# Longformer attention and a snake MLP on one core: the third block of w_in issued behind the casts, and batch 1's global rows turned a group sooner and placed ahead of w_out

## The chip, the cores and the metric

The kernel runs on one core of a Trainium2 chip. The metric is device microseconds of one execution. Before the change three runs gave 374.94 us as the median (374.66 to 376.61).

## The reference

For 8 batches of 8 heads, 576 positions and head dimension 64, attention is computed with a mask that keeps a band of 32 positions to either side, and all rows and columns of 8 global positions. Its output, turned to 4608 tokens of 512, goes through a two-layer network with a snake-like activation.

```python
scores = scale * np.matmul(q, k.transpose(0, 1, 3, 2))
mask = np.abs(pos[:, None] - pos[None, :]) <= window
mask = mask | is_global[:, None] | is_global[None, :]
attn = softmax(np.where(mask, scores, -1e9))     # in the reference written out
x = np.matmul(attn, v)                           # then (4608, 512)
h = x @ w_in                                     # (512, 2048)
g = h + np.sin(alpha * h) ** 2 / (alpha + 1e-9)
out = g @ w_out                                  # (2048, 512)
```

## The kernel before

**Stages.** The program is unrolled by hand, in an order written out in Python; each engine executes its instructions in that order. Attention of batch 0 comes first (`phase_a(0, None)`). Then for each batch b comes `gemm1(b)`, the first matrix product with its activation, and beside the attention of batch b+1 the second product of batch b, `gemm2(b)`, of which single matmuls are dealt out by `fill(n)`.

**Attention.** Keys lie in `KX[b % 2]` and queries in `QX[b % 2]`, both in a layout of 12 blocks of 48 positions, where each block also holds the 8 global keys, or 4 global queries to either side. For each of 4 pairs of heads (hp), three score groups of 4 blocks are computed (L741) into two PSUM buffers in turn (`ring`), exponentiated by ACT (L749) and masked by DVE (L752). Then follow the products with V (L783, key 0, into zn) and with ones (key 1, into zd), the inverse of the sums on ACT as a logarithm and an exponential (L809, L812), and DVE's normalisation (L815), which frees zn for the next pair. In batches 0 and 1 spare matmuls (`warm`, L545) are put between the scores. In batch 1 no matmul of `gemm2(0)` comes before the third pair (`LATE`).

**The first product.** `gemm1(b)` goes through 16 groups (nt) of 128 columns of `w_in`. A group is 8 matmuls (L990) into one of four PSUM places; for batch 0 the places are, in order, `nrdonrdonrdnrdon`, where n, r, d and o are zn, zr, zd and the two halves of zo. Then follow a sine on ACT (L1020), a square on ACT or DVE (L1024, L1026), and the sum on DVE into H (L1028), which frees the place. For batch 0 the squares of groups 1, 3, 5, 7 and 9 to 14 are on ACT. In groups 10 to 13 of batch 0, DVE also places keys and queries of batch 1's first two pairs of heads (`place`, L356 and L349); the other pairs' are placed by `place_rest` after the first pair of batch 1's attention.

**Global rows.** SP gathers the global rows of k, q and v for all batches (`gather`, L488), in float32 into parts of H. `turn_kq` (L697) transposes those of k and q on PE into `zo[1]`, and DVE copies them to `kTg` and `qTg` (L707). `cast_globals_v` (L695) casts those of v on POOL. `place_globals(b)` (L366) copies the global keys of batch b into KX, in 8 copies of 64x96, one for each pair and half, and the global queries into QX in 2 copies of 128x112; all these run on POOL. The attention of batch 1 reads both.

**POOL's queue.** POOL issues all transfers that cast to bfloat16: V (`load_v`, L393, four for each pair of heads), k and q to DRAM (`cast_qk`, L330; SP then transposes them back by DMA, L339, into `kt` and `qt`), `w_in` in four blocks of 512 columns (L410, block g serves groups 4g to 4g+3), and `w_out` in four quarters (L416, in the order in which `gemm2` uses them). Before the change its order after the start is: blocks 0 and 1 of `w_in` between the V loads of batch 0; `cast_qk(1)`; three memsets of batch 1's buffers; a 1x1 copy into `seen` which reads `kt` and so holds POOL until that transpose has landed (L1118); blocks 2 and 3 of `w_in` (L1119); half of batch 1's V; then, emitted at group 11 of `gemm1(0)`, `w_out`, the cast of V's global rows, `place_globals(1)`, the other half of batch 1's V, and after that `cast_qk(2)` and batch 2's V.

**SP's queue** has, in the same stretch: the gather of q, the two transposes of batch 1, the gather of v, and `load_vg`, which spreads the global rows of V (L402).

Of the kernel before, what the change touches and what calls it, by code (L numbers as in the profile page):

```python
# [18 lines left out]
NG = 8  # L19
KT = 48  # L20
# [227 lines left out]
def kernel(  # L248
# [12 lines left out]
    B, H, S, D = q.shape  # L261
# [3 lines left out]
    NT12 = S // KT  # L265
    NHP = H // 2
# [26 lines left out]
    KX = [main.tile([P, NHP, NT12, P], DT.bfloat16, name=f"KX{i}") for i in range(2)]  # L293
# [9 lines left out]
    kTg = main.tile([P, NHP, NG, B], DT.bfloat16, name="kTg")  # L303
# [21 lines left out]
    def cast_qk(b):  # L325

        cast[b] = []
        for src, name in ((k, "kd"), (q, "qd")):
            t = dramp.tile([P, H * S * D // P], DT.bfloat16, name=name)
            nc.gpsimd.dma_start(  # L330
                out=t[:], in_=src[b].rearrange("h s d -> (h s d)").rearrange("(p f) -> p f", p=P)
            )
            cast[b].insert(0, t)
# [31 lines left out]

    def place_globals(b):  # L366

        for hp in range(NHP):
            for t in range(2):
                rows = slice(t * D, (t + 1) * D)  # L370
                nc.gpsimd.tensor_copy(
                    out=KX[b % 2][rows, hp, :, t * D + KT : t * D + KT + NG],
                    in_=kTg[rows, hp, None, :, b].to_broadcast([D, NT12, NG]),
                )
        for y in range(2):
            nc.gpsimd.tensor_copy(
                out=globals_of(b, slice(0, P), y),
                in_=qTg[:, :, None, y::2, b].to_broadcast([P, NHP, 7, 4]),
            )
# [8 lines left out]
    def load_v(b, hps=range(NHP)):  # L388
        for hp in hps:
            for t in range(2):  # L390
                for y in range(2):
                    r = t * D + y * 24
                    nc.gpsimd.dma_start(  # L393
                        out=VX[b % 2][r : r + 24, hp, :, t * D : t * D + D],
                        in_=v[b, 2 * hp + t].rearrange("(i a y) d -> y a i d", a=24, y=2)[y],
                    )

    def load_vg(b):
        for h in range(H):
            t = h % 2  # L400
            src = VGb[b::B, h * D : (h + 1) * D] if b else VG0[h::H]
            nc.sync.dma_start(  # L402
                out=VX[b % 2][t * D + KT : t * D + KT + NG, h // 2, :, t * D : t * D + D],
                in_=src[:, None, :].to_broadcast([NG, NT12, D]),
            )

    def load_w_in(gs):
        for g in gs:
            cols = slice(g * DFF // 4, (g + 1) * DFF // 4)
            nc.gpsimd.dma_start(  # L410
                out=w_in[:, :, cols], in_=moe_w_in[:, cols].rearrange("(c p) n -> p c n", p=P)
            )

    def load_w_out():
        for g in range(4):
            nc.gpsimd.dma_start(  # L416
                out=w_out[:, 4 * g : 4 * g + 4, :],
                in_=moe_w_out[4 * g * P : (4 * g + 4) * P, :].rearrange("(t p) n -> p t n", p=P),
            )
# [21 lines left out]
    for half in range(2):  # L441
        for w, src in ((1, k), (0, q)):
            nc.gpsimd.dma_start(
                out=nat[w][D * half : D * half + HK],
# [23 lines left out]
    for t in (gidx8, gp64):  # L468
        nc.vector.memset(t[:].bitcast(DT.int32), 0)
    nc.sync.dma_start(  # L470
        out=g64[:],
# [4 lines left out]
    for t in (0, D):  # L476
        nc.sync.dma_start(out=gp64[t + KT : t + KT + NG], in_=global_idx[:, None])
        nc.sync.dma_start(
            out=gidx8[t + KT : t + KT + NG],
# [82 lines left out]
    load_w_in((1,))  # L562
    load_v(0, (3,))
    cast_qk(1)
    load_vg(0)
    gather(q, gq)

# [399 lines left out]
    def gemm1(b):  # L967


        xT = xTs[b]  # L970
        r0 = (b % 2) * S
        more = b == B - 1
        W = HALF + (NE if more else 0)
        hr = tc.alloc_tile_pool(name="hr", bufs=1, space=PSUM)
        hs = {}

        order = "nrdonrdonrdnrdon" if b == 0 else "nrd" * 5 + "n"

        def chunks(nt, cs):
            if nt not in hs:  # L980
                if order[nt] == "o":
                    hs[nt] = [(slice(e, e + 1), zo[e][:, None, :]) for e in range(2)]
                else:
                    h = {"n": zn, "d": zd}.get(order[nt]) or hr.tile([P, 2, 512], DT.float32, name="zr")
                    hs[nt] = [(slice(0, 2), h[:])]
            h = [ap[:, i] for es, ap in hs[nt] for i in range(es.stop - es.start)]
            for c in cs:
                for e in range(2):
                    lhsT = w_in[:, c, nt * P : (nt + 1) * P]
                    nc.tensor.matmul(  # L990
                        out=h[e][:, 0:W], lhsT=lhsT, rhs=xT[:, c, e, 0:W],
                        start=(c == 0), stop=(c == CT - 1), skip_group_check=True,
                    )

        on_act = (ON_ACT_FIRST, ON_ACT_SECOND, ON_ACT)[min(b, 2)]
        for nt in range(NT):
            if b < 2 and 10 <= nt < 14:
                for which, t, y in PLACES[2 * (nt - 10) : 2 * (nt - 9)]:
                    place(b + 1, which, t, y, nc.vector.tensor_copy, slice(0, NHP if b else 2))
            if b == 1 and nt in (3, 4):  # L1000
                square_x(0, nt - 3)
            if b == 0 and nt == 11:
                turn_kq()
            if b == 0 and nt == 11:

                load_w_out()
                cast_globals_v()
                place_globals(1)
                load_v(1, (2, 3))
                load_vg(1)  # L1010
            if nt == 0:

                for n in range(2):
                    chunks(n, range(CT - 1))
            chunks(nt, range(CT - 1, CT) if nt < 2 else range(CT))
            fill((GROUP_LATE if b == 1 else PER_GROUP)[nt])
            sb = spool.tile([P, 2, HALF + NE], DT.bfloat16, name="sb")
            s2 = spool.tile([P, 2, HALF + NE], DT.bfloat16, name="s2")
            for es, h in hs[nt]:
                nc.scalar.activation(  # L1020
                    out=sb[:, es, 0:W], in_=h[:, :, 0:W], func=AF.Sin, scale=alphaT[:, nt : nt + 1]
                )
            if nt in on_act:
                nc.scalar.activation(out=s2[:, :, 0:W], in_=sb[:, :, 0:W], func=AF.Square)  # L1024
            else:
                nc.vector.tensor_tensor(out=s2[:, :, 0:W], in0=sb[:, :, 0:W], in1=sb[:, :, 0:W], op=ALU.mult)  # L1026
            for es, h in hs[nt]:
                nc.vector.scalar_tensor_tensor(  # L1028
                    out=H2[:, nt, r0 : r0 + S].rearrange("p (e c) -> p e c", e=2)[:, es],
                    in0=s2[:, es, 0:HALF], scalar=recipT[:, nt : nt + 1], in1=h[:, :, 0:HALF],  # L1030
                    op0=ALU.mult, op1=ALU.add,
                )
            if more:
                nc.vector.scalar_tensor_tensor(
                    out=HG[:, nt, :].rearrange("p (x n) -> p x n", x=2),
                    in0=s2[:, :, HALF:W], scalar=recipT[:, nt : nt + 1], in1=hs[nt][0][1][:, :, HALF:W],
                    op0=ALU.mult, op1=ALU.add,
                )
        hr.release()
# [65 lines left out]
    def phase_a(b_att, b_moe):  # L1105
        def beside(at):

            if b_moe is None:
                if at == -1:
                    nc.vector.tensor_scalar(out=recipT[:], in0=alphaT[:], scalar1=1e-9, scalar2=None, op0=ALU.add)  # L1110
                    nc.vector.reciprocal(out=recipT[:], in_=recipT[:])
                if at == 0:
                    second_half()
                    nc.gpsimd.memset(VX[1][:].bitcast(DT.int32), 0)
                    nc.gpsimd.memset(QX[1][:].bitcast(DT.int32), 0)
                    nc.gpsimd.memset(KX[1][:].bitcast(DT.int32), 0)
                    turn_qk(1)
                    nc.gpsimd.tensor_copy(out=seen[:], in_=turned[1][1][0:1, 0:1])  # L1118
                    load_w_in((2, 3))  # L1119
                    load_v(1, (0, 1))  # L1120
                    gather(v, gv)
                return
            if 0 <= at < 2 and b_moe:
                square_x(b_moe, at)
            if b_att == 1 and at == 0:
                place_rest(1)
                place_rest(0)
            for which, t, y in places_at(b_att, at):
                place(b_att + 1, which, t, y, nc.vector.tensor_copy)
            if b_moe == 0 and at == 2:  # L1130
                turn_qk(2)

        if b_moe is not None:
            waiting.append(gemm2(b_moe))
        attention(b_att, beside)
# [77 lines left out]
```

## Time and profile before

| | |
|---|---|
| median of three runs | 374.94 us |
| profiled execution | 374.3 us |
| its span, first to last instruction | 372.6 us |
| mean granted PE clock | 0.986 |
| PE busy | 338.7 us (91%) |
| ACT busy | 293.9 us (79%) |
| DVE busy | 282.8 us (76%) |
| POOL busy | 138.3 us (37%) |
| `gemm1(0)`: first and last L990 matmuls start | 31.97 and 50.95 us |
| attention of batch 1: first scores | 54.05 us |
| `gemm1(1)`: first L990 matmuls | 71.67 us |

The span begins with the first instruction and ends with the last; the profiled execution's time is 1.7 us above it. Busy shares are taken over the whole span, though the stretch that the change touches lies between 23 and 75 us, and is read from the timelines, which merge neighbouring instructions of one kind: start, duration, engine, line, what is written and read, their number, and in brackets the idle time ahead of them and what ended it. A transfer's row on POOL is its issue; the time to its landing is counted from the issue's start: 6.1 and 8.6 us for blocks 2 and 3 of `w_in`, 5.9, 8.0, 9.7 and 12.0 us for the quarters of `w_out`, 7.2 and 9.1 us for the casts of k and q of batch 1.

### The profile page before, as it was taken

How to read it: one execution, taken by the hardware profiler on the slowest of the kernel's cores; microseconds unless marked ns; L12 is line 12 of the kernel's file. 1: busy time of each engine (PE TensorE's matmuls, PEld its weight loads, DVE VectorE, ACT ScalarE, POOL GpSimd, SP SyncE). 2: the span in 40 equal slices, each digit the busy share in tenths (PEclk: the TensorE clock that was granted, in tenths of full speed). 3: DMA queues.
4: the chain of work that ended last, by engine and by line, in shares of the span. 5: the costliest groups of instructions: out<-in, count | busy, mean ns of one | idle time of the engine just before them, and what ended most of it. 6: DMA issues, size and time to landing. Idle time of an engine off the chain costs nothing. (4 is left out here: it accounts for less than half of the span.)

```text
span 372.6 us, 8428 instructions
## 1 busy us (share of the span) xinstructions
PE 338.7 (91%) x3040; PEld 228.7 (61%) x3040; DVE 282.8 (76%) x621; ACT 293.9 (79%) x566; POOL 138.3 (37%) x246
## 2 busy tenths in 40 slices
PE   1678769999998999999999999999999999994993
PEld 1567546766576766767676756776667666551441
DVE  6777897598878787888788878888878776888240
ACT  7799897888878788878888888888888988788110
POOL 7894596669844604470357016700000000000001
PEclk9999998999999999999999999999999999998998
DMA  6999999999999586966498517626100000101211
GB/s 120 115 158 209 152 155 184 147 186 187 154 210 213 35 157 100 160 98 90 68 175 119 84 58 67 65 46 143 30 28 30 23 35 31 31 0 35 75 61 52
DMA packets 103579, 38.07 MB, mean 102 GB/s; under 512 B 94138, under 2 KB 98250, under 8 KB 103082
## 3 DMA queue, kind: packets, MB, share of 16 engines
q0 software_dynamic: 56640, 18.56, 43.9%
q1 hardware_dynamic: 46890, 18.89, 24.4%
q8 instruction: 26, 0.43, 0.5%
q14 instruction: 23, 0.19, 0.2%
HBM read 37.15 MB, written 17.83 MB: 148 GB/s over the span
## 5 line engine op out<-in xcount | busy, mean ns | idle before, releaser
L1047 PE MATMUL zo<-w_out,H 128*128 128x512 bf16 x576 | 155.4, 382 | 4.9 <-ACT osb L1053 4.9
L990 PEld LDWEIGHTS <-w_in 128*128 128x128 bf16 x1024 | 98.6, 98 | 47.7 <-issue 10.3
L393 POOL DMA_DIRECT2D VX<-in_v_dram x128 | 83.2, 662 | 92.7 <-PE zd L783 60.9
L1047 PEld LDWEIGHTS <-H 128*128 128x128 bf16 x576 | 52.6, 98 | 43.4 <-issue 7.2
L749 ACT ACTIVATE E<-ring 128x480 bf16<-128x480 f32 x96 | 54.3, 568 | 21.8 <-PE ring L741 21.4
L752 DVE TENSOR_TENSOR E<-E,MASK 128x480 bf16<-128x480 bf16 x96 | 35.9, 404 | 16.8 <-ACT E L749 15.5
L1075 POOL DMA_INDIRECT out_dram<-osb,grow x1 | 1.0, 998 | 126.9 <-DVEq L1181 126.9
L1028 DVE SCALAR_TENSOR_TENSOR H<-s,recipT,zn 128x576 bf16<-128x576 bf16 x47 | 38.2, 813 | 10.0 <-ACT s L1024 6.2
L1024 ACT ACTIVATE s<-sb 128x576 bf16<-128x576 bf16 (+1 forms) x62 | 42.7, 689 | 2.0
L1020 ACT ACTIVATE sb<-zn,alphaT 128x576 bf16<-128x576 f32 (+1 forms) x47 | 34.8, 740 | 11.6 <-PE zn L990 11.6
L741 PE MATMUL ring<-QX,KX 128*128 128x120 bf16 x384 | 37.8, 224 | 6.3 <-ACT E L749 3.3
L741 PEld LDWEIGHTS <-KX 128*128 128x128 bf16 x384 | 28.8, 101 | 21.9 <-issue 10.3
L1028 DVE SCALAR_TENSOR_TENSOR H<-s,recipT,zd 128x576 bf16<-128x576 bf16 x39 | 31.7, 813 | 6.6 <-ACT s L1024 4.7
L1028 DVE SCALAR_TENSOR_TENSOR H<-s,recipT,zr 128x576 bf16<-128x576 bf16 x39 | 31.7, 812 | 4.6 <-ACT s L1024 2.5
L1053 ACT COPY osb<-zo 128x512 f32<-128x512 f32 x36 | 20.7, 578 | 17.8 <-PE zo L1047 14.8
L1026 DVE TENSOR_TENSOR s<-sb 128x576 bf16<-128x576 bf16 (+1 forms) x66 | 30.6, 464 | 5.2 <-ACT sb L1020 4.9
L1020 ACT ACTIVATE sb<-zd,alphaT 128x576 bf16<-128x576 f32 (+1 forms) x39 | 28.9, 741 | 7.2 <-PE zd L990 5.6
L1020 ACT ACTIVATE sb<-zr,alphaT 128x576 bf16<-128x576 f32 (+1 forms) x39 | 28.9, 741 | 5.6 <-PE zr L990 5.6
L783 PEld LDWEIGHTS <-VX 128*128 128x128 bf16 x448 | 26.3, 99 | 9.3 <-issue 3.1
L990 PE MATMUL zn<-xT,w_in 128*128 128x288 bf16 x184 | 26.9, 286 | 4.2 <-DMA w_in<-in_moe_w_in_dram 2.0
L990 PE MATMUL zn<-xlast,w_in 128*128 128x288 bf16 (+1 forms) x192 | 28.8, 289 | 0.3
L783 PE MATMUL zn<-E,VX 128*128 128x120 bf16 (+2 forms) x336 | 26.6, 210 | 1.0 <-DVE xlast L815 0.9
(159 smaller groups left out, 488.3 us busy)
## 6 DMA issues: line engine op xcount, KB each, us to landing
VX<-in_v_dram POOLq DMA_DIRECT2D x128, 36.0 KB, 5.6
kd<-in_k_dram POOLq DMA_DIRECT2D x7, 576.0 KB, 7.2
qd<-in_q_dram POOLq DMA_DIRECT2D x7, 576.0 KB, 9.2
w_in<-in_moe_w_in_dram POOLq DMA_DIRECT2D x4, 512.0 KB, 6.5
w_out<-in_moe_w_out_dram POOLq DMA_DIRECT2D x4, 512.0 KB, 8.9
out_dram<-osb SPq DMA_DIRECT2D x8, 256.0 KB
out_dram<-osb SPq DMA_DIRECT2D x8, 224.0 KB
out_dram<-osb SPq DMA_DIRECT2D x8, 192.0 KB
```

The source lines that it names most:

```text
L393: nc.gpsimd.dma_start(out=VX[b % 2][r : r + 24, hp, :, t * D : t * D + D], in_=v[b, 2 * hp + t].rearrange("(i a y) d -> y a i d", a=24, y= ...
L741: nc.tensor.matmul(out=ps[:, e * WCOL : (e + 1) * WCOL], lhsT=kx[:, hp, i, :], rhs=qx[:, hp, :, s0 : s0 + 60], start=True, stop=True, skip ...
L749: nc.scalar.activation(out=Eg, in_=ps[:, 0 : 4 * WCOL], func=AF.Exp, scale=scale, accum_out=EA[:, n : n + 1])
L752: nc.vector.tensor_tensor(out=Eg, in0=Eg, in1=MASK[:, 4 * g : 4 * g + 4, :].rearrange("p i c -> p (i c)"), op=ALU.mult,)
L783: nc.tensor.matmul(out=out_t[:, half, :, a - half * CUT : z - half * CUT], lhsT=OB[:] if key else VXb[:, hp, i, :], rhs=E[:, i, :, a - s0 ...
L990: nc.tensor.matmul(out=h[e][:, 0:W], lhsT=lhsT, rhs=xT[:, c, e, 0:W], start=(c == 0), stop=(c == CT - 1), skip_group_check=True,)
L1020: nc.scalar.activation(out=sb[:, es, 0:W], in_=h[:, :, 0:W], func=AF.Sin, scale=alphaT[:, nt : nt + 1])
L1024: nc.scalar.activation(out=s2[:, :, 0:W], in_=sb[:, :, 0:W], func=AF.Square)
L1026: nc.vector.tensor_tensor(out=s2[:, :, 0:W], in0=sb[:, :, 0:W], in1=sb[:, :, 0:W], op=ALU.mult)
L1028: nc.vector.scalar_tensor_tensor(out=H2[:, nt, r0 : r0 + S].rearrange("p (e c) -> p e c", e=2)[:, es], in0=s2[:, es, 0:HALF], scalar=recip ...
L1047: nc.tensor.matmul(out=ops[:], lhsT=H2[:, nt, blk * P : (blk + 1) * P], rhs=w_out[:, nt, :], start=(nt == 0), stop=(nt == NT - 1),)
L1053: nc.scalar.copy(out=osb[:], in_=ops[:])
```

## The change

There are three edits.

- Block 2 of `w_in` (groups 8 to 11) is issued by POOL directly after `cast_qk(1)`, ahead of the memsets and of the copy into `seen`; block 3 stays where it was.
- At group 10 of `gemm1(0)` instead of 11, `turn_kq` is emitted, ahead of the group's matmuls and behind its two placements. Then come `cast_globals_v` and `place_globals(1)`, and only then `w_out`, which had been ahead of both. What follows `w_out` keeps its order.
- For batch 1 `place_globals` copies the keys of all four pairs of heads at once: two copies of 64x384 in place of eight of 64x96. The queries' two copies and all other batches are unchanged.

```diff
     def place_globals(b):
 
-        for hp in range(NHP):
+        step = NHP if b == 1 else 1
+        for hp in range(0, NHP, step):
+            hps = slice(hp, hp + step)
             for t in range(2):
                 rows = slice(t * D, (t + 1) * D)
                 nc.gpsimd.tensor_copy(
-                    out=KX[b % 2][rows, hp, :, t * D + KT : t * D + KT + NG],
-                    in_=kTg[rows, hp, None, :, b].to_broadcast([D, NT12, NG]),
+                    out=KX[b % 2][rows, hps, :, t * D + KT : t * D + KT + NG],
+                    in_=kTg[rows, hps, None, :, b].to_broadcast([D, step, NT12, NG]),
                 )
...
     load_v(0, (3,))
     cast_qk(1)
+    load_w_in((2,))
     load_vg(0)
     gather(q, gq)
...
-            if b == 0 and nt == 11:
+            if b == 0 and nt == 10:
                 turn_kq()
-            if b == 0 and nt == 11:
-
-                load_w_out()
                 cast_globals_v()
                 place_globals(1)
+                load_w_out()
                 load_v(1, (2, 3))
                 load_vg(1)
...
                     nc.gpsimd.tensor_copy(out=seen[:], in_=turned[1][1][0:1, 0:1])
-                    load_w_in((2, 3))
+                    load_w_in((3,))
                     load_v(1, (0, 1))
                     gather(v, gv)
```

## The prediction

> **What bounds the kernel now.** I read the page's busy shares first: PE is busy for 338.7 of 372.6 us, so time is to be had only where PE stands still or runs slowly. The waits list two such places that the diff touches, 2.0 us for a block of `w_in` and 2.0 us for QX from POOL. So next the timelines of PE, ACT, DVE and POOL between 30 and 75 us, where both lie (start, duration, engine and line; idle time ahead of a row and its releaser in brackets). First PE:
>
> ```profile
> 42.22 1.15 PE L990 MATMUL zn<-xT,w_in 128*128 128x288 bf16 x8 [1.95 <-DMA w_in<-in_moe_w_in_dram]
> ...
> 54.05 0.37 PE L741 MATMUL ring<-QX,KX 128*128 128x120 bf16 x4 [1.96 <-POOL QX L376]
> ...
> 65.94 1.02 PE L1047 MATMUL zo<-w_out,H 128*128 128x512 bf16 x4
> ```
>
> Together 3.9 us, 1% of the span. But PE isn't the engine that is behind here. ACT:
>
> ```profile
> 43.41 0.74 ACT L1020 ACTIVATE sb<-zn,alphaT 128x576 bf16<-128x576 f32 x1 [1.21 <-PE zn L990]
> 44.39 0.74 ACT L1020 ACTIVATE sb<-zr,alphaT 128x576 bf16<-128x576 f32 x1 [0.24 <-PE zr L990]
> ...
> 53.39 1.28 ACT L725 ACT_TABLE_LOAD   x1
> 54.68 0.57 ACT L749 ACTIVATE E<-ring 128x480 bf16<-128x480 f32 x1
> ...
> 60.15 0.74 ACT L809 ACTIVATE L<-zd,tiny 128x576 f32<-128x576 f32 x1
> ```
>
> ACT has no gap between 32.6 us and the first exponential but these 1.21 + 0.24 = 1.45 us. Its table load ends at 54.67, after the first scores are there (54.05 + 0.37 = 54.42). So **PE's wait for QX costs nothing by itself** (cover 0.25 us), and the wait for `w_in` costs 1.45 us at most. DVE and POOL:
>
> ```profile
> 42.28 0.93 DVE L1028 SCALAR_TENSOR_TENSOR H<-s,recipT,zo 128x288 bf16<-128x288 bf16 x2
> ...
> 49.63 0.41 DVE L707 CAST qTg<-zo 128x256 bf16<-128x256 f32 x1
> ...
> 59.82 1.04 DVE L752 TENSOR_TENSOR E<-E,MASK 128x480 bf16<-128x480 bf16 x3
> ...
> 61.73 0.76 DVE L815 TENSOR_TENSOR xlast<-zn,R 128x576 bf16<-128x576 f32 x1 [0.45 <-ACT R L812]
> ```
>
> ```profile
> 46.53 3.04 POOL L416 DMA_DIRECT2D w_out<-in_moe_w_out_dram x4
> ...
> 50.12 3.13 POOL L371 COPY KX<-kTg 64x96 bf16<-64x96 bf16 x8
> 53.31 0.69 POOL L376 COPY QX<-qTg 128x112 bf16<-128x112 bf16 x2
> ```
>
> Behind the first exponentials PE is slow; the stretch's fields are PE, PEld, DVE, ACT, POOL, then the granted clock:
>
> ```profile
> 55.30:58.70 3.40, 3.31 (x25) 2.49 (x25) 3.33 (x9) 2.58 (x9) 3.22 (x6) 0.51 1.34 211
> ```
>
> **Part 1, `w_in`'s third block behind the casts.** POOL issues it at 24.2 us (0.79 us, as at 36.1), ahead of the three memsets. POOL then idles 5.13 us for kt, which covers 0.79 us; without that cover, everything from the fourth block on would be 0.79 us later. At 36 us one issue of 0.79 us goes. The V loads of L1120 move up, and the second last of the eight no longer waits for the third block: in the trace a V load waits for the transfer issued eight before it (42.46 after 36.06, 45.74 after 36.84). The last of them then waits for the fourth block alone: 36.06 + 6.1 = 42.2 us, so POOL is free at 42.8 instead of 46.4. The block lands by some 24.5 + 9 to 12 us (qd took 9.1 from the same spot), long before group 8, which can then start when zn is free, at 40.35 instead of 42.22. ACT goes on at 42.20: at most 1.45 us gained.
>
> **Part 2, the turn a group sooner.** The eight transposes of `turn_kq` now stand in PE's queue ahead of group 10, and they write `zo[1]`, which group 7 gives back when DVE's two L1028 end: 42.28 + 0.93 = 43.21. That doesn't move, since ACT's square of group 7 ends at 42.20 in either kernel. Groups 8 and 9 are done at 42.4, so PE waits 0.8 us here; behind the wait stand group 10 and all that follows. Transposes 0.65 us (45.26 to 45.91 in the trace), group 10 from 43.9 to 45.05, its sine at 45.1 instead of 45.75. **So 0.65 of the 1.45 us remain.** From there ACT is back to back: 0.65 us carry to the table load, which ends at 54.02. PE ends group 15 near 50.7.
>
> **Part 3, the globals.** DVE's casts move from behind group 11's placements to behind group 10's: kTg at 46.4, qTg at 46.8. The cast of VGb needs `gather(v)`, issued by SP until 43.0; no row shows its landing, but POOL's sequencer passed those waits by 48.2. So the cast starts between 43 and 48.2, I take 46 or before. Two key copies of 64x384 aren't in the trace: all linear in 64x96 they cost 4 x 0.39 = 1.56 us each, by the VGb cast (0.63 us for 512) 0.47. I take 1.0, from the 1x1 copy (0.18 us) plus four times the rest of 0.39: 2.0 instead of 3.13 us. QX done at 46.4 + 2.0 + 0.69 = 49.1 (48.0 to 50.2), far ahead of the 53.6 at which the scores would begin to hold ACT.
>
> **Part 4, `w_out` behind it.** Its first issue T moves from 46.53 to 49.1. Its last quarter landed at 60.8, 14.3 us after T, and is needed at 65.94; if PE comes 0.9 us sooner, the slack is 4.2, so T may rise to 50.7 for nothing. The last V load for batch 1 waits for that quarter (61.06, landed 4.6 later) and is needed at 71.05: slack 4.5. The casts for batch 2 go from 61.7 to some 64; the placements that use them run after 88 us. V globals on SP go sooner with the cast. All at nothing, given that T.
>
> **Part 5, what 0.65 us become.** Between the first exponential and the first logarithm (60.15) PE is the limit, at the granted 0.51. If the half-clock stretch stays at 55.3 to 58.7 (PE was busy 1.30 of the 3.4 us before; my new timeline has about 1.25), the second pair's scores start at 55.3 instead of 56.17, but the last 0.47 us before 59.13, which ran at full clock, now run at half: the gain shrinks to 0.4. If the clock stays up, DVE is the limit: masks till 56.1, `place_rest` 2.75, masks 1.04, sums 0.3, so the normalisation starts at 60.3, not 61.73: 1.45. I take the middle, **0.9 us**, with both ends. Each later pair of heads repeats at 4.27 us, and from 71.7 us PE runs back to back, so this reaches the end.
>
> The Trainium skill (TensorE: Matmul & The Clock Gate, "What's actually happening") says that the clock falls to half after at least one idle window of about 3.4 us, in free-running windows. This trace differs: half clock came after a stretch with 1.30 us of work and a single gap of 1.96 us, so the measurement decides; by the page alone no clock would be there to win, and the gain would be the 0.65.
>
> Sum: 374.3 - 0.9 = 373.4 for the profiled execution. The median of the runs, 374.94, is 0.6 above it; I state 373.9, leaning to the runs.
>
> **Rivals.**
> A. Both PE waits come off whole: 374.94 - 3.9 = 371.0. For it: both are in the trace. Against: ACT's unbroken row of work, and `zo[1]`. 12%.
> B. The edit doesn't do what it says: PE's stall only moves from the block to the transposes, and the rest is lost at half clock: 374.6 to 375.2. For it: the 43.21 of `zo[1]`. 15%.
> C. **Slower: `w_out` too late.** Part 1 puts a block of 1 MB read beside the DMA transposes (30.4 to 36); the qt transpose holds SP, and `gather(v)` stands behind it, then the VGb cast, the copies, and T. If the gather lands at 48.2 and the copies take 2.0, T is 48.2 + 0.63 + 2.0 + 0.69 = 51.5; each us of delay adds one. From T = 50.7 on PE waits for the last quarter; from 51.6 the gain is gone; a delay of 2 us more gives T = 53.5, 1.9 us behind zero, 376.8. Against it: seen's 35.83 and the gap of POOL. 15%.
> The Trainium skill (Trainium Kernel Development and Optimization, "Key Constraints") states that transfers issued from SP and POOL share the same 16 DMA engines and interleave, which speaks for C; before, this block was never beside the transposes, so no row here shows the price.
> My forecast keeps 58%.
>
> **Numbers.** About 0.5%, 1.87 us, is what a measurement can tell from no change. Faster needs under 373.07: A (12%) and the upper part of the forecast (its 1.45 and the spread of the runs, 374.66 to 376.61), 16%: 28%. Slower: most of C, 12%. The rest, 60%, is the same. The range 372.4 to 375.8 leaves out A's far end and C's tail; the forecast's own is 373.0 to 374.6.
>
> **What would show it.** Right: no wait for `w_in` ahead of group 8; a PE wait at the transposes released by DVE H, near 0.8 us; ACT's table load starting near 52.7; QX copies done by 50.2; no PE wait at L1047. Wrong: a wait for `w_out` or VX between 58 and 70, VGb's cast after 48, key copies over 1.6 us each, or kt landing after 38.

## The result, and the profile after

The changed kernel takes 380.12 us (median of 6 runs, 378.1 to 382.12); the kernel before took 375.62 in the same comparison (6 runs, 373.68 to 379.37). The ratio is 1.0128, with a 95% interval of 1.008 to 1.0177: **4.5 us slower**. Forecast was 373.9, within 372.4 to 375.8.

The wait for `w_in` went as meant, the one for QX stayed; then others came. First POOL's timeline, of the kernel before and then of the changed one (start, duration, line; idle time ahead and its releaser in brackets; the changed file's lines are up to three further down):

```profile
35.83 0.18 POOL L1118 COPY seen<-kt 1x1 bf16<-1x1 bf16 x1 [5.13 <-DMA kt<-kd]
...
49.56 0.63 POOL L695 CAST VGb<-H 64x512 bf16<-64x512 f32 x1
```

```profile
38.94 0.18 POOL L1119 COPY seen<-kt 1x1 bf16<-1x1 bf16 x1 [7.37 <-DMA kt<-kd]
...
46.47 0.65 POOL L395 DMA_DIRECT2D VX<-in_v_dram  x1 [2.00 <-DMA w_in<-in_moe_w_in_dram]
50.35 0.60 POOL L698 CAST VGb<-H 64x512 bf16<-64x512 f32 x1 [3.23 <-DMA H<-in_v_dram]
50.91 1.78 POOL L373 COPY KX<-kTg 64x384 bf16<-64x384 bf16 x2
52.75 0.69 POOL L378 COPY QX<-qTg 128x112 bf16<-128x112 bf16 x2
53.39 3.03 POOL L418 DMA_DIRECT2D w_out<-in_moe_w_out_dram  x4
```

kt lands 3.1 us later than the 35.83 of before. Then a wait stands there that the trace of before didn't have: the cast of V's global rows waits 3.23 us for the gather of v. Behind it in POOL's queue are the keys, the queries and now `w_out`, whose first issue goes from 46.53 to 53.39. SP's timeline, again before and changed, shows where kt's delay is from; its first transpose held SP for 5.94 us, against 3.20 before, and the gather of v behind it began at 39.17 instead of 36.13:

```profile
30.39 3.20 SPq L339 DMA_TRANSPOSE kt<-kd  x1
...
36.13 6.87 SPq L488 DMA_DIRECT2D H<-in_v_dram  x8
```

```profile
30.48 5.94 SPq L339 DMA_TRANSPOSE kt<-kd  x1
36.53 2.45 SPq L339 DMA_TRANSPOSE qt<-qd  x1
39.17 7.55 SPq L490 DMA_DIRECT2D H<-in_v_dram  x8
```

What late `w_out` does is read on PE's timeline of the changed kernel:

```profile
43.59 0.87 PE L706 MATMUL zo<-idf,H 64*128 64x64 f32 x8 [0.74 <-DVE H L1029]
...
53.49 0.37 PE L744 MATMUL ring<-QX,KX 128*128 128x120 bf16 x4 [2.46 <-POOL QX L378]
...
62.12 0.38 PE L1048 MATMUL zo<-w_out,H 128*128 128x512 bf16 x1 [0.84 <-DMA w_out<-in_moe_w_out_dram]
...
65.95 1.02 PE L1048 MATMUL zo<-w_out,H 128*128 128x512 bf16 x4 [1.02 <-DMA w_out<-in_moe_w_out_dram]
...
68.73 1.02 PE L1048 MATMUL zo<-w_out,H 128*128 128x512 bf16 x4 [1.55 <-DMA w_out<-in_moe_w_out_dram]
70.92 0.36 PE L786 MATMUL zn<-E,VX 128*128 128x88 bf16 x4 [1.17 <-DMA VX<-in_v_dram]
...
75.80 0.90 PE L993 MATMUL zn<-xlast,w_in 128*128 128x288 bf16 x6
```

Before, that last row was:

```profile
71.67 0.90 PE L990 MATMUL zn<-xlast,w_in 128*128 128x288 bf16 x6
```

No wait for `w_in` is left ahead of group 8. The transposes wait 0.74 us for DVE. PE stands for QX even longer than before (2.46 us), and that costs nothing. ACT's first exponential comes at 54.51, 0.17 sooner than before. Then four new waits, 0.84 + 1.02 + 1.55 + 1.17 = 4.58 us, three for quarters of `w_out` and one for V. `gemm1(1)` begins at 75.80 instead of 71.67: 4.1 us are lost in this one stage. The profiled spans differ by 5.8 us; 1.4 of that lies in the last 35 us, where the same 26 matmuls of `w_out` took 8.64 instead of 7.27 us because PE ran at half clock there for 6.8 us instead of 3.4. In the profiles of e1 and e10 below they took 8.28 and 7.97 us, without a loss in the ratios, so this part isn't put down to the change.

The transfers themselves were hardly slower. The quarters of `w_out` landed 6.1 to 13.0 us after their issue, against 5.9 to 12.0 before. They began late, and until then little else moved, as the last field of a stretch shows (what the transfers moved, in GB/s), before and then changed:

```profile
52.00:53.00 1.00, 0.10 (x1) 0.00 (x0) 0.96 (x3) 0.97 (x3) 0.88 (x4) 1.00 1.11 180
```

```profile
52.00:53.00 1.00, 0.00 (x0) 0.10 (x1) 0.99 (x2) 1.00 (x2) 0.94 (x2) 1.00 0.10 13
```

From 51 to 54 us the three stretches of 1 us moved 156 to 180 GB/s before and 8 to 23 in the changed kernel.

### The profile page after: what moved, and what is told of

Its sections match the earlier page's. It is cut to its first block, busy times and chain, and to the rows that moved or that the text cites. A ratio compares the mean times of both kernels' runs of the same rounds, so it can differ in the third digit from the quotient of the medians.

```text
span 378.4 us, 8421 instructions
## 1 busy us (share of the span) xinstructions
PE 340.9 (90%) x3040; PEld 229.1 (61%) x3040; DVE 283.4 (75%) x621; ACT 293.8 (78%) x566; POOL 138.1 (36%) x240
## 5 line engine op out<-in xcount | busy, mean ns | idle before, releaser
L755 DVE TENSOR_TENSOR E<-E,MASK 128x480 bf16<-128x480 bf16 x96 | 36.2, 405 | 21.6 <-ACT E L752 20.2
L1054 ACT COPY osb<-zo 128x512 f32<-128x512 f32 x36 | 20.7, 578 | 19.1 <-PE zo L1048 16.1
```

The costliest lines, as they stand in the source:

```text
L755: nc.vector.tensor_tensor(out=Eg, in0=Eg, in1=MASK[:, 4 * g : 4 * g + 4, :].rearrange("p i c -> p (i c)"), op=ALU.mult,)
L1054: nc.scalar.copy(out=osb[:], in_=ops[:])
```

## The experiments

Each ran in five rounds against the kernel before. For comparison, all in one table. "Issue" is POOL's first issue of `w_out`; "waits" are PE's waits from 56 us on for `w_out`, for V or for V's global rows; "to exp" is the time from ACT's first load of the sine table to batch 1's first exponential, and "exp to sine" from there to the next load of the sine table, both from one profiled execution. The waits of e4 and e8 are put down to V by what they stand ahead of; their rows name DVE and `w_out` as releasers.

| kernel | ratio to before (95%) | issue | waits | to exp | exp to sine |
|---|---|---|---|---|---|
| before | 1 | 46.5 | 0 | 22.1 | 17.4 |
| changed | 1.0128 (1.008 to 1.0177) | 53.4 | 4.6 | 21.6 | 21.7 |
| e1_block_only | 0.9996 (0.9972 to 1.0019) | 47.1 | 0.2 | 21.2 | 17.0 |
| e2_order_only | 1.009 (1.0062 to 1.0118) | 52.8 | 2.9 | 21.6 | 19.9 |
| e3_wout_first | 0.9993 (0.9967 to 1.002) | 45.7 | 0 | 21.7 | 18.2 |
| e4_cast_last | 1.0098 (1.0061 to 1.0135) | 49.3 | 2.8 | 21.6 | 21.3 |
| e5_gather_first | 1.0137 (1.0108 to 1.0166) | 53.2 | 2.6 | 22.2 | 19.6 |
| e6_swap_only | 1.0152 (1.0126 to 1.0178) | 53.8 | 3.8 | 21.8 | 22.0 |
| e7_both_blocks | 1.0048 (1.0022 to 1.0075) | 49.5 | 0 | 21.8 | 17.3 |
| e8_halves | 1.0033 (1.0012 to 1.0055) | 47.7 | 0.4 | 21.1 | 18.6 |
| e9_own_rows | 1.003 (1.001 to 1.005) | 50.3 | 0 | 21.6 | 18.5 |
| e10_rows_wout_first | 1.0009 (0.9989 to 1.0028) | 46.1 | 0 | 20.7 | 16.7 |
| e11_turn_copies | 1.0014 (0.9989 to 1.0039) | 47.2 | 0 | 21.6 | 17.1 |

**The block alone.**

```diff
     cast_qk(1)
+    load_w_in((2,))
     load_vg(0)
...
-                    load_w_in((2, 3))
+                    load_w_in((3,))
```

> The kernel before with one edit: block 2 of w_in issued right behind the casts. Theory G (the block runs beside the DMA transposes, holds SP there, and so makes the gather of v late; the loss comes from w_out, which waits behind that gather): kt lands near 38.9 us instead of 35.8 and the cast of V's global rows waits until about 50.4, but w_out is still ahead of the cast and issued near 47, so PE does not wait at L1047. The keys follow the cast (3.1 us), the queries end near 54.9, the first exponential comes at 55.4 instead of 54.7: ratio 1.000 to 1.004. Rival H (the block's own traffic slows the whole start, w_out or not): ratio 1.01 or more. Rival T (the loss is the turn a group sooner): no kt delay, ratio 0.996 to 1.000.

Measured: no change that can be told (0.9996); the times of theory G came, its small loss didn't. SP and POOL of this kernel:

```profile
31.23 5.93 SPq L339 DMA_TRANSPOSE kt<-kd  x1
37.26 2.15 SPq L339 DMA_TRANSPOSE qt<-qd  x1
39.60 6.76 SPq L488 DMA_DIRECT2D H<-in_v_dram  x8
```

```profile
39.35 0.18 POOL L1119 COPY seen<-kt 1x1 bf16<-1x1 bf16 x1 [6.99 <-DMA kt<-kd]
...
47.14 0.78 POOL L416 DMA_DIRECT2D w_out<-in_moe_w_out_dram  x1
48.20 2.24 POOL L416 DMA_DIRECT2D w_out<-in_moe_w_out_dram  x3 [0.27 <-DMA VX<-in_v_dram]
50.41 0.65 POOL L696 CAST VGb<-H 64x512 bf16<-64x512 f32 x1
```

The block beside the transposes stretches the first one from 3.20 to 5.93 us, so this delay is the block's doing. Over all profiles it took 4.7 to 6.3 us with the block beside it, and 2.2 to 3.5 without. But the cast, at the same 50.4 as in the changed kernel, has no wait ahead of it, since `w_out`'s issue fills the time. Theory H (the block's traffic costs by itself) falls.

**Order, turn and copies without the block**: the changed kernel with the block's edit undone.

> The changed kernel without the move of block 2: the turn at group 10, the globals ahead of w_out and the two key copies alone. Theory G: kt lands near 35.8, the gather of v is there by 48.2, the first w_out is issued at 49.5 to 50.7, PE waits less than 0.5 us in all at L1047, and the wait of 2 us for block 2 is back: ratio 0.997 to 1.003. Rival O (the order of globals and w_out is the loss by itself, w_out being late in any case): w_out issued after 52, over 2 us of waits at L1047, ratio 1.007 or more.

Measured 1.009: theory G fails in one point and rival O is nearer. POOL:

```profile
36.16 0.18 POOL L1118 COPY seen<-kt 1x1 bf16<-1x1 bf16 x1 [5.60 <-DMA kt<-kd]
...
49.80 0.60 POOL L697 CAST VGb<-H 64x512 bf16<-64x512 f32 x1 [3.29 <-DMA H<-in_v_dram]
...
52.83 3.03 POOL L418 DMA_DIRECT2D w_out<-in_moe_w_out_dram  x4
```

kt is early, yet the cast waits till 49.80. So the gather of v, whose last issue ends at 43.28 here, releases the cast only 6.5 us later. In the changed kernel its last issue ends at 46.72 and the cast goes 3.6 us later: 3.4 us more in the issue move the cast by 0.5 us. What sets the landing isn't shown; the block's part in it is this 0.5 us. In the kernel before, a landing near the same time would be hidden by `w_out`'s 3.04 us of issue: its cast began at 49.56 without a wait. The run after next tests that.

**`w_out` back in front.**

```diff
                 turn_kq()
+                load_w_out()
                 cast_globals_v()
                 place_globals(1)
-                load_w_out()
```

> The changed kernel with w_out put back ahead of the cast and the globals. Theory G: kt as late as in the changed kernel (38.9), w_out issued near 47.1, no wait for w_out and none for the V loads at 66 to 72 us; the cast waits for the gather until 50.4, the queries end near 53.5 as in the changed kernel and the first exponential is at 54.5: ratio 0.996 to 1.001, so the whole loss goes. Rival H (the block's traffic): a ratio of 1.008 or more stays.

Measured 0.9993: the whole loss goes with this one line, and nothing is gained. The counterpart is the swap in the kernel before, alone:

```diff
-                load_w_out()
                 cast_globals_v()
                 place_globals(1)
+                load_w_out()
```

> The kernel before with one edit: w_out issued behind the cast and the globals instead of ahead of them; the block, the turn and the eight key copies as before. Theory G2: w_out's issue had hidden the wait for the gather, so the cast waits until 49.8, the first w_out comes at 54.2 and its last quarter 14 us later at 68: waits of 4 to 6 us at L1047 and for the V loads behind, ratio 1.010 to 1.017, most of the changed kernel's loss from this edit alone. Rival B (the block behind the casts is needed for the loss): ratio under 1.005.

Measured 1.0152: at least as much as the whole change, whose interval reaches over it. `w_out` came at 53.78, behind a cast that waited 2.76 us until 49.44:

```profile
49.44 0.60 POOL L695 CAST VGb<-H 64x512 bf16<-64x512 f32 x1 [2.76 <-DMA H<-in_v_dram]
...
53.78 3.03 POOL L416 DMA_DIRECT2D w_out<-in_moe_w_out_dram  x4
```

With e3 this settles the cause: it is `w_out`'s place behind the cast and the globals, in either kernel. The transfers agree: from 51 to 54 us they moved 12 to 25 GB/s in e2 and e6, and 148 to 199 in e1 and e3.

**The cast behind `w_out`**, so that neither globals nor `w_out` wait for the gather:

```diff
                 turn_kq()
-                cast_globals_v()
                 place_globals(1)
                 load_w_out()
+                cast_globals_v()
```

> The changed kernel with only the cast of V's global rows moved behind w_out, so that neither the globals nor w_out wait for the gather of v. Theory G: the keys start near 47.1, the queries end near 49.6, w_out is issued near 49.7, that is before 50.7, and PE waits under 0.5 us at L1047; the cast comes near 52.7. The first exponential is bound by ACT at 54.5 or sooner: ratio 0.995 to 1.000. Rival (w_out waits for something else than the gather, such as the DMA engines): waits over 2 us at L1047 stay, ratio 1.006 or more.

Half of it came: `w_out` was issued at 49.34 and PE waited nowhere for it. Yet the ratio was 1.0098. PE:

```profile
60.48 0.53 PE L786 MATMUL zn<-E,VX 128*128 128x88 bf16 x4 [2.80 <-DVE E L755]
```

The releaser named is DVE's masking, which for this pair had ended at 56.98, so it was something else. The candidate is V's global rows: with the cast last, SP begins to spread them at 53.02, against 50.21 in the kernel before. (PE's half clock came on top in this profile: three stretches in a row, 10.2 us.) To test it, batch 1 got these rows by an indirect gather of its own, spread right behind the gather of v, with e4's order kept (the gather and its index tile are new; later batches still use the cast):

```diff
+    nc.gpsimd.indirect_dma_start(
+        out=VG1[:], out_offset=None, in_=v.rearrange("b h s d -> (b h s) d"),
+        in_offset=bass.IndirectOffsetOnAxis(ap=grow1[:, 0:1], axis=0),
+    )
...
                     gather(v, gv)
+                    load_vg(1)
...
-                load_vg(1)
```

> As the run with the cast last (changed kernel, cast of V's global rows behind w_out), but batch 1's global rows of V come from an indirect gather of their own on POOL, issued behind block 2, and SP spreads them right behind the gather of v, so nothing of batch 1 waits for the cast. Theory G3 (there, w_out was in time and the 2.8 us that PE stood ahead of batch 1's first products were for V's global rows): that wait falls under 0.3 us, w_out is again issued near 49.5 with no wait at L1047, the first exponential is at 54.5 to 54.9: ratio 0.996 to 1.001. Rival (the 2.8 us were DVE's masks, as the profile's releaser says, or w_out's traffic): the wait stays and the ratio is 1.006 or more.

The 2.80 us wait is gone, and with it most of the loss: 1.003. So **two things hung on the gather of v, not one**: `w_out`, in POOL's queue, and the global rows on SP. And with `w_out` issued at 50.34 PE didn't wait for it. What the rest of the loss is stays open. One candidate is the clock: in this kernel's profile PE ran at half clock for two stretches in a row (the fields as before, the granted clock third from the end), 6.8 us instead of the 3.4 in the kernel before. That it is the rest of the loss is not shown, and e3 speaks against it: its profile has two such stretches as well, at a ratio of 0.9993.

```profile
55.70:62.50 6.80, 6.02 (x53) 4.85 (x53) 5.30 (x15) 4.15 (x14) 2.79 (x5) 0.52 1.27 201
```

**The gather of v ahead of the transposes**, on SP, in the changed kernel:

```diff
+                    gather(v, gv)
                     turn_qk(1)
...
                     load_v(1, (0, 1))
-                    gather(v, gv)
```

> The changed kernel with one edit on SP: the gather of v is issued ahead of batch 1's two transposes instead of behind them. Theory G2 (what makes w_out late is the landing of this gather, some 6 us after its last issue; the block beside the transposes adds only part): the cast of V's global rows no longer waits (3.2 us in the changed kernel), the keys start by 48, w_out is issued by 51, waits for w_out at L1047 fall from 3.4 us to under 0.5, kt lands at 41 to 42 and delays the V loads by 2 us: ratio 0.996 to 1.001. Rival (w_out behind the globals is late even without that wait): over 1.5 us of waits at L1047 and a ratio over 1.005.

```profile
42.94 0.20 POOL L1120 COPY seen<-kt 1x1 bf16<-1x1 bf16 x1 [11.60 <-DMA kt<-kd]
...
49.25 0.65 POOL L395 DMA_DIRECT2D VX<-in_v_dram  x1 [0.67 <-DMA w_in<-in_moe_w_in_dram]
49.89 0.63 POOL L698 CAST VGb<-H 64x512 bf16<-64x512 f32 x1
...
53.15 3.11 POOL L418 DMA_DIRECT2D w_out<-in_moe_w_out_dram  x4
```

A miss, of use all the same. The cast doesn't wait any more, but kt lands four us later, the V loads stand behind it, and `w_out` is issued at 53.15, 0.24 us sooner than in the changed kernel, at the same loss (1.0137). The loss isn't `w_out`'s alone here, for PE also waited 1.16 us for the fourth block of `w_in`, behind the late kt. Still, with no wait of the cast, the late issue again goes with PE's waits for `w_out` (1.92 us) and V (0.71): what makes `w_out` late doesn't matter; that it is late does.

**The turn and the copies alone**, with `w_out` in front and the block where it was.

> The kernel before with the turn at group 10 and the two key copies alone; w_out stays ahead of the cast and the globals, the block stays where it was. All theories that put the loss on w_out behind the globals: w_out issued at 46.5, no wait at L1047, ratio 0.998 to 1.003; the wait for w_in (2 us) stays and the transposes wait under 0.5 us for DVE. If the ratio is 1.005 or more, the turn itself costs.

Measured 1.0014, an interval about 1: as expected, neither part costs or brings anything that can be told. The wait for `w_in` was 1.08 us in its profile, not 2.

**Three attempts at a better kernel.** The first puts blocks 2 and 3 behind the casts and the gather of v ahead of the transposes, and takes the turn back to group 11, followed by cast, `w_out` and globals.

> A version meant to beat both: blocks 2 and 3 of w_in behind the casts, the gather of v ahead of the transposes, the turn back at group 11, then the cast, w_out, and the globals with two key copies. Theory G2: no wait for w_in, the cast does not wait, w_out is issued near 48, the queries end near 53.3, the first exponential comes at 53.5 to 54 instead of 54.7 and nothing waits for V's global rows: ratio 0.996 to 1.000. Rival (the start is bound by DMA work as a whole, so what one transfer wins another loses): kt lands after 43, the placements hold DVE, ratio 1.000 to 1.006.

It is slower, 1.0048, as its rival had it: kt landed at 43.18, the V loads ended at 48.95, the queries at 55.0, and PE stood 3.50 us for them. The second splits block 2 into halves in its old place, with the two key copies.

> The kernel before with block 2 of w_in issued as two halves of 256 columns from the same place, and two key copies; order and turn as before. The wait for w_in falls from 2.0 to under 1 us. Theory G3 (there is a second deadline behind the gather of v: the global rows of V, which SP spreads after the cast, land some 7 us after their first issue, near 57.8, just when the first pair's products need them): the cast still waits until 49.6 or later, PE waits up to 1.4 us ahead of the first products of batch 1, ratio 0.998 to 1.002. Rival A (the wait for w_in comes off in full): first exponential 1.2 us sooner and no wait ahead of the products, ratio 0.995 to 0.998.

Slower as well, 1.0033, just above what either theory allowed. The wait for `w_in` fell to 0.42 us and the first exponential came after 21.1 instead of 22.1 us; then PE waited 2.98 us for the queries and 0.38 ahead of the first products, and again ran two stretches at half clock. The third takes all that the others taught:

```diff
-            if b == 0 and nt == 10:
+            if b == 0 and nt == 11:
                 turn_kq()
-                cast_globals_v()
-                place_globals(1)
                 load_w_out()
+                place_globals(1)
+                cast_globals_v()
```

with the block behind the casts, two copies, and batch 1's own global rows as in e9.

> The attempt at a version that beats both: block 2 behind the casts, the global rows of V from their own gather, the turn back at group 11, w_out first, then the globals in two key copies, the cast last. Theory G3: no wait for w_in over 0.3 us, queries done by 52.8, table load from 52 to 53.3, first exponential by 53.6 (1.1 us sooner than before), no wait for w_out or V: ratio 0.993 to 0.998. Rival D (the half-clock stretch and DVE's placements behind the first exponentials take the gain back, as part 5 of the prediction had as its lower end): 0.998 to 1.001.

Even with before (1.0009). In its profile ACT reaches the first exponential after 20.7 us, 1.4 less than before, which is the whole of ACT's gap; there is no stretch at half clock and no wait for a transfer. Still `gemm1(1)` begins at 71.30 there, only 0.4 us ahead of the kernel before, since `gemm1(0)` began at 33.67 instead of 31.97. No version beat the kernel before.

## Why the prediction was wrong, point by point

**What bounds the stage.** "PE's wait for QX costs nothing by itself" held: the changed kernel's PE waits longer for QX than before and its exponential isn't later; e1's 2.72 us of it cost ACT 0.46.

**Part 1.** The block landed 12.0 us after its issue, and group 8 didn't wait: right. "At nothing" for POOL's later queue was wrong: POOL was to be free at 42.8 and was free at 47.1, for the block beside the transposes made kt land 3.1 us late. This was named only in rival C. The Trainium skill (Trainium Kernel Development and Optimization, "Key Constraints") says that transfers issued from SP and POOL share the DMA engines and interleave; the runs agree, with 5.93 us for the transpose beside the block against 3.20 without. By itself that cost nothing in time, as e1 shows.

**Part 2.** Right: 0.8 us of waiting for `zo[1]` forecast, 0.74 measured; 0.65 us left to ACT forecast, 0.5 measured (22.1 to 21.6). The 0.5 can't be put down to the block, however: e11, with the block in its old place, came to 21.6 as well. The size of the prize had been taken from one execution. The block's landing is set by the transfers, and PE's arrival by when `gemm1(0)` begins. ACT's first load of the sine table was at 32.58 in the profile of before, and between 32.9 and 34.4 in all others; in e6, e11 and e2, which leave the block in place, it was at 33.46, 33.91 and 34.23, and PE's wait for `w_in` was 1.68, 1.08 and 0.41 us. The 1.95 us were the longest of the four, and the profiled execution of before (374.3 us) lies 1.3 us under that kernel's median in the comparison (375.62). What moves that start wasn't tried; one row goes with it. The spare matmuls of batch 0's attention (L545) fall from 0.63 to 0.38 us at 24.66 in before, and in e2, whose program is the same up to there, from 0.63 at 25.36 to 0.41 only at 27.33.

**Part 3 is the step that failed.** "POOL's sequencer passed those waits by 48.2. So the cast starts between 43 and 48.2", and 46 or before was taken. It began at 50.35, so T, the first issue of `w_out`, was 53.39 and not 49.1. Four short semaphore rows of 48.2 to 48.5 had been read as a landing; e2 and e6 show that the gather isn't there before 49.4 to 49.8 even where the block isn't moved. In the kernel before, the 3.04 us in which POOL issued `w_out` covered this wait, as e6 shows by taking them away, and the trace showed none: the cast stood behind `w_out` by order, and began at 49.56 because POOL came to it then. The edit took the cover away. The copies were right: 0.89 us each, 1.0 forecast.

**Part 4** drew the line well: T up to 50.7 for nothing. `w_out` issued at 45.7 to 50.3 had no wait for it at L1047 (e1, e3, e4, e7 to e11), at 52.8 and later always (e2, e5, e6, the changed kernel). But it priced too little behind the line. Rival C had T = 53.5, measured 53.39, and 1.9 us of loss; it was 4.5. Missing were the V loads of batch 1's last two pairs, which lie in the same queue behind `w_out`: the first four, issued from 56.38 to 59.2, landed 12.0 to 13.1 us after their issues, where before they took some 7.4. Only the very last of these loads had been counted. And each quarter that is late stops PE in order, with the attention's matmuls behind it, so that the quarters' waits add up instead of overlapping.

**Part 5** can be read up to the first logarithm, which lies ahead of these waits. Counted from ACT's first load of the sine table it came after 27.14 us, against 27.57 before: 0.43 us sooner. The half clock stayed, 55.7 to 59.1, and for that case 0.4 had been forecast; the 0.9 that went into the sum was not there by then. The other case, without half clock, and what would have reached the end stay open.

**The chances.** Rival C, which named what came, had been given 15%, because of one landing time for which no row stood. That its T of 53.5 lies so near the measured 53.39 is in part luck: it added an assumed delay of 2 us, which it put to the block beside the transposes, to a landing at 48.2. The block's part was 0.5 us (e2 against the changed kernel), and the gather was 1.6 us later than 48.2 without it. Of the four signs of being wrong, three came: the waits for `w_out` and VX, the cast after 48, and kt after 38.

## What to carry to other kernels

Before moving a long issue out of the way of something, ask what it hides: an instruction behind it that shows no wait may only never have been early enough to wait. A landing without a row is to be taken as unknown, bounded by its first user on one side only, and the result for its late end is to be worked out in full, with every transfer in the same queue behind it. And the size of a wait between two chains that start apart isn't given by one profile: the wait for `w_in` was 1.95, 1.68, 1.08 and 0.41 us in four that left it alone.

## What the runs showed of the hardware that wasn't expected

A small transfer can land long after its issue: the 8 issues of the gather of v were over at 43.28 in e2 and the cast could go at 49.80, 6.5 us later. Traffic ahead of it doesn't explain all of that, for from 48 us on the transfers moved at most 8 GB/s there. The changed kernel shows what large transfers ahead do: the first V loads behind `w_out`, 36 KB each, took 12.0 to 13.1 us, and the last, issued at 68.97 when the last quarter had landed, took 2.6 us.

The half clock comes in steps of 3.4 us, and their number in this stage differed between near equal orders: none in e10 and e11, one in the kernel before, the changed one, e1, e2, e5 and e7, two in a row in e3, e8 and e9, two apart in e6, and three in a row in e4. From the first exponential to the next sine table, those with at most 0.4 us of waits took 16.7 and 17.1 us with none, 17.0 to 17.4 with one (e1, e7, before), and 18.2 to 18.6 with two. So one step can't be told from none here, while two go with about 1 us more. The Trainium skill (TensorE: Matmul & The Clock Gate, "What's actually happening") names at least one idle window of about 3.4 us as what lowers the clock. The length of the stretches agrees; the cause is not so simple here, since before's came with 1.30 us of work in the 3.4 us ahead of it.
